# Moving a relay from SyncE to GpSimd and the loads and stores of GpSimd to SyncE, with longer DMA transposes and 4-byte taps, in a convolution + SwiGLU kernel

## The chip, the cores and the metric

One core of a Trainium2 chip. The metric is the device time of one execution in microseconds (us), lower is better.

## The reference, cut to what matters

```python
# x (8, 4096, 192), weight (8 heads, 7 taps); w_gate, w_val (192, 1536), w_out (1536, 192)
w = softmax(weight, axis=-1)
out = causal 7-tap convolution of x along the sequence, one filter per head of 24 channels
x = out.reshape(32768, 192)
g = x @ w_gate
return (g * sigmoid(g) * (x @ w_val)) @ w_out          # float32
```

## The kernel before

The 32768 rows are worked on in 64 blocks of 512 rows. Two blocks make a unit; 32 units. One unit has 24 steps (12 groups of 128 hidden columns, for each of two blocks). In each step PE does six matmuls (gate and val, 64 of its 128 rows each, in alternation), ACT does a Silu (g * sigmoid(g)), DVE multiplies. Between them stand bursts of matmuls that use the two halves ("row tiles") of the array for different banks of PSUM, the memory that takes PE's results: the out projection in two of three steps, and the convolution of the next unit in steps 0, 3, 6 and 9. After each burst the halves swap banks, and the first matmul of the next burst may only start when the last one is finished. This is what the relay is for: a no-op on another engine that waits for the last matmul and that the next burst waits for.

```python
    def after_relay(mm):
        last_mm[0] = mm
        if relay[0] is not None:
            tc.add_manual_dep(mm.ins, relay[0].ins.name, SYNC, reason="row tiles swap banks")
            relay[0] = None

    def emit_relay():
        relay[0] = nc.sync.nop(nofuse=True)
        tc.add_manual_dep(relay[0].ins, last_mm[0].ins.name, SYNC, reason="row tiles swap banks")
```

The convolved unit goes from SBUF (`stage`) to a DRAM scratch (`xc`) and comes back transposed (`xq`), 64 channels on each half of the partitions. Both are DMAs that SyncE issues, in program order with the relays. Loads of x (which cast to fp16 as they go) and stores of the output are issued by GpSimd. At the start, the filter taps are placed in `toep` ("toeplitz"), banded matrices with which PE does the convolution as matmuls.

```python
    def emit_to_dram(b):                       # the "scratch store"
        ...
        nc.sync.dma_start(out=dr.rearrange("(g r) d -> r g d", r=G), in_=conv[u][i * Q : i * Q + G])

    def emit_transpose(b, i):                  # six a block, RP = 256 rows each
        ...
        r, q = i // NQ * RP, i % NQ
        nc.sync.dma_start_transpose(
            out=xqs[b][:, q, r : r + RP], in_=drs[b][r : r + RP, q * Q : q * Q + P])
    ...
    # in the loop over steps s of a unit (cut):
        if burst and live:
            emit_relay()
        ...
            if s in (11, 12):
                emit_to_dram((u + 1) * UB + s - 11)
            if 17 <= s < 17 + 2 * NQ:
                emit_transpose((u + 1) * UB, s - 17)      # first block of the next unit
        if live and s < 2 * NQ:
            emit_transpose(u * UB + 1, s)                 # second block of this unit
```

Of the kernel before, what the change touches and what calls it, by code (L numbers as in the profile page):

```python
# [11 lines left out]
def kernel(  # L12
# [9 lines left out]
    nc = tc.nc  # L22
    fp32 = mybir.dt.float32
    fp16 = mybir.dt.float16
    i32 = mybir.dt.int32
    u16 = mybir.dt.uint16
    AF = mybir.ActivationFunctionType
    ALU = mybir.AluOpType
    AX = mybir.AxisListType
# [2 lines left out]
    B, S, D = x.shape  # L32
    H, K = weight.shape
    NT = B * S
    Dff = moe_w_gate.shape[1]
    P = 128
    grp = D // H
    SUBS = 4
    TB = P * SUBS
    NCH = Dff // P  # L40
    pad = K - 1

    Q = 64
    NQ = D // Q
    G = 57
    UG = 9
    UB = 2
# [1 line left out]
    XD = D + Q  # L49
    TR = 3  # L50
    F2_LAG = TR + 1
    RP = TB // 2
    SCALE = 1024.0

    assert D == NQ * Q and NQ == 3 and UB == 2 and UG * G >= TB
# [5 lines left out]
    n_units = NT // UT  # L61
    upb = S // UT

    x_flat = x.flatten_outer_dims()

    const_pool = ctx.enter_context(tc.tile_pool(name="const", bufs=1))
# [8 lines left out]


    last_rows = TB - ((UG - 1) * G - pad)
    x16s = []
    for i in range(2):
        x16 = const_pool.tile([P, UG, D], fp16, tag=f"x16_{i}", name=f"x16_{i}")  # L80
        nc.gpsimd.memset(x16[Q:P, UG - 1, :], 0.0)
        x16s.append(x16)

    def windows(t, rows, n):
        return bass.AP(
            tensor=x_flat.tensor, offset=t * D, ap=[[D, rows], [G * D, n], [1, D]]
        )

    def emit_fetch(u):
        x16 = x16s[u % 2]  # L90
        t0 = u * UT - pad
        if u % upb == 0:
            nc.gpsimd.memset(x16[0:pad, 0, :], 0.0)
            nc.gpsimd.dma_start(out=x16[pad:Q, 0, :], in_=x_flat[t0 + pad : t0 + Q, :])
            nc.gpsimd.dma_start(out=x16[0:Q, 1:UG, :], in_=windows(t0 + G, Q, UG - 1))
        else:
            nc.gpsimd.dma_start(out=x16[0:Q, :, :], in_=windows(t0, Q, UG))  # L97
        tb = t0 + TB
        nc.gpsimd.dma_start(  # L99
            out=x16[Q:P, 0 : UG - 1, :], in_=windows(tb, Q, UG - 1)  # L100
        )
        tl = tb + (UG - 1) * G
        nc.gpsimd.dma_start(  # L103
            out=x16[Q : Q + last_rows, UG - 1, :], in_=x_flat[tl : tl + last_rows, :]
        )

    man = tc.manual_schedule(engines={EN.PE, EN.SP, EN.Activation, EN.DVE, EN.Pool})
    ctx.enter_context(man)
# [4 lines left out]
        out=wraw, in_=bass.AP(tensor=weight.tensor, offset=0, ap=[[0, P], [K, H], [1, K]])  # L113
# [8 lines left out]
    FS = Dff // 4  # L122
    wg_v = moe_w_gate.rearrange("(q p) f -> p q f", p=Q)
    wv_v = moe_w_val.rearrange("(q p) f -> p q f", p=Q)
    wo_v = moe_w_out.rearrange("(c p) d -> p c d", p=P)
    for f in range(0, Dff, FS):
        fs = slice(f, f + FS)
        cs = slice(f // P, (f + FS) // P)
        nc.sync.dma_start(out=w_st[0:Q, :, fs], in_=wg_v[:, :, fs])
        nc.sync.dma_start(out=w_st[Q:P, 0 : NQ - 1, fs], in_=wv_v[:, 1:NQ, fs])  # L130
        nc.sync.dma_start(out=w_st[Q:P, NQ - 1, fs], in_=wv_v[:, 0, fs])
        nc.sync.dma_start(out=wo_st[:, cs, :], in_=wo_v[:, cs, :])


    diag = const_pool.tile([P, G], i32, tag="diag", name="diag")
    for lo in (0, Q):
        nc.gpsimd.iota(diag[lo : lo + Q], pattern=[[-1, G]], base=0, channel_multiplier=1)
    band = const_pool.tile([P, H, 2, G], fp16, tag="band", name="band")
    nc.gpsimd.memset(band, 0.0)
    toep = const_pool.tile([P, H, 2, P], fp16, tag="toep", name="toep")  # L140
    nc.gpsimd.memset(toep, 0.0)
    masks = []
    for k in range(K):
        mask = const_pool.tile([P, G], u16, tag=f"mask{k}", name=f"mask{k}")
        nc.vector.tensor_scalar(mask, diag, scalar1=k, scalar2=None, op0=ALU.is_equal)
        masks.append(mask)

# [17 lines left out]
    nc.vector.tensor_tensor(  # L165
        wn, wexp, wsum.unsqueeze(2).to_broadcast([P, H, K]), op=ALU.mult
    )
    whl = const_pool.tile([P, H, 2, K], fp16, tag="whl", name="whl")
    nc.vector.tensor_copy(whl[:, :, 0], wn)
    nc.vector.tensor_tensor(whl[:, :, 1], wn, whl[:, :, 0], op=ALU.subtract)  # L170
    for h in range(0, H, 4):
        hs = slice(h, h + 4)
        for k in range(K):
            nc.vector.copy_predicated(  # L174
                band[:, hs].rearrange("p h c m -> p (h c) m"),
                masks[k].unsqueeze(1).to_broadcast([P, 8, G]),
                whl[:, hs, :, k : k + 1]
                .rearrange("p h c k -> p (h c) k")
                .to_broadcast([P, 8, G]),
            )  # L180

        nc.vector.tensor_copy(toep[0:Q, hs, :, 0:G], band[0:Q, hs])  # L182
        nc.vector.tensor_copy(toep[Q:P, hs, :, Q : Q + G], band[Q:P, hs])

    def emit_weight_cast(i):
        fs = slice(i * FS, (i + 1) * FS)
        cs = slice(i * FS // P, (i + 1) * FS // P)
        nc.scalar.copy(w_r[:, :, fs], w_st[:, :, fs])
        nc.gpsimd.tensor_copy(wo_r[:, cs, :], wo_st[:, cs, :])

    emit_weight_cast(0)

    SYNC = mybir.DependencyInfo(mybir.DependencyClass.Sync, mybir.DependencyReason.DATA)
    relay = [None]
# [7 lines left out]

    def emit_relay():

        relay[0] = nc.sync.nop(nofuse=True)  # L205
        tc.add_manual_dep(
            relay[0].ins, last_mm[0].ins.name, SYNC, reason="row tiles swap banks"
        )
# [51 lines left out]

    xqs = {}

    def emit_transpose(b, i):

        if i == 0:
            xqs[b] = xpool.tile([P, NQ, TB], fp16, tag="xq", name="xq")
        r, q = i // NQ * RP, i % NQ
        nc.sync.dma_start_transpose(  # L268
            out=xqs[b][:, q, r : r + RP], in_=drs[b][r : r + RP, q * Q : q * Q + P]
        )  # L270

    def emit_gv(j, xq):
# [55 lines left out]
    def emit_store(b, acc):  # L328
        t0 = b * TB
        o_sb = opool.tile([P, SUBS, D], fp32, tag="o_sb", name="o_sb")  # L330
        nc.scalar.copy(o_sb[:, 0:2, :], acc[0])  # L331
        nc.vector.tensor_copy(o_sb[:, 2:4, :], acc[1])  # L332
        nc.gpsimd.dma_start(  # L333
            out=out[t0 : t0 + TB, :].rearrange("(s p) d -> p s d", p=P), in_=o_sb
        )

    for fill in range(2):
        for phase in range(2):
# [4 lines left out]
        if fill == 0:  # L343
            emit_dup(0)
    emit_to_dram(0)
    for i in range(2 * NQ):
        emit_transpose(0, i)
    emit_to_dram(1)
    for i in range(1, 4):
        emit_weight_cast(i)  # L350
    if n_units > 1:
        emit_fetch(1)

    hlists, accs = {}, {}
    ns = NCH * UB
    for g in range(n_blocks * NCH + F2_LAG):
        b, j = divmod(g, NCH)
# [28 lines left out]
        if burst and live:  # L386
            emit_relay()
        if g >= F2_LAG and fj == NCH - 2:
            emit_store(fb, accs.pop(fb))
        if live:  # L390
            emit_h(sj, ps, hlists[b])
        if g >= F2_LAG and fj == NCH - 1:
# [1 line left out]
        if more:  # L394
            if s in (3, 4, 9, 10):
                emit_conv_out(u + 1, s // 6, s % 3)
            if s == 5:
                emit_dup(u + 1)
                if u + 2 < n_units:
                    emit_fetch(u + 2)  # L400
            if s in (11, 12):
                emit_to_dram((u + 1) * UB + s - 11)
            if 17 <= s < 17 + 2 * NQ:
                emit_transpose((u + 1) * UB, s - 17)
        if live and s < 2 * NQ:
            emit_transpose(u * UB + 1, s)


# [28 lines left out]
```

## Time and profile before

| | before |
|---|---|
| time, median of 2 runs | 1077.84 us |
| first Silu | 41.2 us |
| one unit, mean (from first Silus of units 0 and 31, 41.19 and 1043.99 us) | 32.35 us |
| PE busy / mean granted clock | 84% / 0.987 |

The page's first part (busy us, share of the span, instructions):

```profile
PE 910.0 (84%) x11752; PEld 562.7 (52%) x11752; DVE 572.8 (53%) x865; ACT 550.1 (51%) x968; POOL 146.5 (14%) x222
```

No engine is full. The page's fourth part, the chain of waits, says who ended last, by engine and by line. SPq is SyncE's queue; L268 is the transpose, L255 the scratch store:

```profile
PE 43%; SPq 32%; DMA 8%; DVE 7%; issue 4%; ACT 4%; POOL 0%; POOLq 0%; ACTq 0%; DVEq 0%
SPq L268 24%; PE gate L278 17%; PE val L278 9%; SPq L255 8%; DVE h L294 4%; ACT sig L289 4%; DVE o_sb L332 2%; DVE band L174 1%; DMA xc_220<-stage 1%; DMA xc_229<-stage 1%; DMA xq<-xc_16634 0%; DMA xq<-xc_11455 0%; SPq L205 0%; DMA xq<-xc_6851 0%; DMA xq<-xc_6276 0%
```

The waits view (who waited for what: us in total, times, longest). L205 is the relay; PE's weight loads wait for it:

```profile
PEld L307 <- SPq L205: 145.4, 168, 3.1
...
PEld L227 <- SPq L205: 25.9, 56, 1.6
```

SyncE's queue in one unit, whose first Silu is at 431.59 and the next unit's at 463.19 (timeline: start, us, engine, line, what, count):

```profile
432.45 8.27 SPq L268 DMA_TRANSPOSE xq<-xc_6865  x6
446.16 0.25 SPq L255 DMA_DIRECT2D xc_7426<-stage  x1
446.46 2.60 SPq L255 DMA_DIRECT2D xc_7440<-stage  x1
453.69 7.89 SPq L268 DMA_TRANSPOSE xq<-xc_7426  x6
```

The transposes are read from the second block's store of the unit before (xc_6865) and from the first block's of the next (xc_7426). The last one of xc_7426 leaves SyncE at 461.58, 1.6 us before the unit begins that needs it. How long one holds SyncE (the view of a line: least, median, longest in ns):

```profile
L268 SPq DMA_TRANSPOSE xq<-xc_1095 x6: 1163/1204/1959, 98.4 to 105.8; - x6
```

The start, from the timeline: first convolution, its second half, scratch store, transposes, first gate matmul, first Silu:

```profile
15.35 0.36 PE L227 MATMUL cps_173<-x_0_82,toep 64*128 64x216 f16 x1 [15.35 <-DVE toep L182]
...
21.69 0.36 PE L227 MATMUL cps_196<-x_0_82,toep 64*128 64x216 f16 x1 [4.13 <-DVE toep L182]
...
25.01 0.34 SPq L255 DMA_DIRECT2D xc_220<-stage  x1
31.76 7.63 SPq L268 DMA_TRANSPOSE xq<-xc_220  x6
38.02 0.60 PE L278 MATMUL gate<-xq,w_sb 64*128 64x512 f16 x1 [14.12 <-DMA xq<-xc_220]
...
41.19 0.60 ACT L289 ACTIVATE sig<-gate 128x512 f16<-128x512 f32 x1 [13.13 <-PE val L278]
```

### The profile page before, as it was taken

The numbers are of one execution on the slowest core, as the hardware profiler recorded it, in microseconds if no ns is written. First come the engines' busy times: TensorE is split into PE (matmuls) and PEld (weight loads), VectorE is DVE, ScalarE is ACT, GpSimd is POOL, SyncE is SP. The second block draws the span as 40 slices with busy tenths as digits, with TensorE's granted clock in tenths as the row PEclk, the third lists the DMA queues.
The fourth block names the chain that finished last, engine by engine and source line by source line (L and its number), as shares of the span: only waits on it lengthen the run. The fifth ranks groups of instructions, "written<-read, shape, count | busy, mean of one in ns | idle before, by whom it ended". The sixth has DMA issues, their size and how long they took to land.

```text
span 1077.4 us, 28716 instructions
## 1 busy us (share of the span) xinstructions
PE 910.0 (84%) x11752; PEld 562.7 (52%) x11752; DVE 572.8 (53%) x865; ACT 550.1 (51%) x968; POOL 146.5 (14%) x222
## 2 busy tenths in 40 slices
PE   1488989888888888998888988888888888988887
PEld 0155655555555555655555555555555555655555
DVE  5155555555555555555555555455555555554555
ACT  2255555554555455555554555455555454554554
POOL 4001111110111101111100111101111101111000
PEclk9999999999999999999999999999999999999999
DMA  9424443423444335444423443333433423443321
GB/s 163 58 66 92 88 83 74 90 78 68 89 75 78 80 69 91 86 82 75 92 69 78 89 83 71 78 79 81 91 83 73 89 71 76 88 82 70 80 72 38
DMA packets 192916, 86.72 MB, mean 80 GB/s; under 512 B 150736, under 2 KB 187664, under 8 KB 192784
## 3 DMA queue, kind: packets, MB, share of 16 engines
q0 software_dynamic: 45696, 39.29, 20.5%
q1 hardware_dynamic: 147088, 45.59, 18.5%
q8 instruction: 92, 1.51, 0.6%
q14 instruction: 40, 0.33, 0.1%
HBM read 31.79 MB, written 41.98 MB: 68 GB/s over the span
## 4 chain that ended last, share of the span: by engine, by line
PE 43%; SPq 32%; DMA 8%; DVE 7%; issue 4%; ACT 4%; POOL 0%; POOLq 0%; ACTq 0%; DVEq 0%
SPq L268 24%; PE gate L278 17%; PE val L278 9%; SPq L255 8%; DVE h L294 4%; ACT sig L289 4%; DVE o_sb L332 2%; DVE band L174 1%; DMA xc_220<-stage 1%; DMA xc_229<-stage 1%; DMA xq<-xc_16634 0%; DMA xq<-xc_11455 0%; SPq L205 0%; DMA xq<-xc_6851 0%; DMA xq<-xc_6276 0%
## 5 line engine op out<-in xcount | busy, mean ns | idle before, releaser
L294 DVE TENSOR_TENSOR h<-sig,val 128x512 f16<-128x512 f16 x768 | 526.2, 687 | 443.5 <-ACT sig L289 386.2
L289 ACT ACTIVATE sig<-gate 128x512 f16<-128x512 f32 x768 | 458.5, 597 | 476.0 <-PE val L278 289.6
L278 PE MATMUL gate<-xq,w_sb 64*128 64x512 f16 x2304 | 645.6, 382 | 53.1 <-DMA xq<-xc_220 15.4
L278 PE MATMUL val<-xq,w_sb 64*128 64x512 f16 x2304 | 634.7, 380 | 18.1 <-DVE h L294 13.1
L307 PEld LDWEIGHTS <-h 64*128 64x128 f16 x6096 | 297.2, 95 | 198.7 <-SPq L205 145.4
L278 PEld LDWEIGHTS <-w_sb 64*128 64x128 f16 x4608 | 263.2, 95 | 250.7 <-issue 107.7
L333 POOL DMA_DIRECT2D out_dram<-o_sb x64 | 49.7, 777 | 855.9 <-ACT o_sb L331 462.0
L227 PEld LDWEIGHTS <-toep 64*128 64x128 f16 x1024 | 49.1, 97 | 59.1 <-SPq L205 25.9
L247 POOL COPY stage<-stage 128x576 f16<-128x576 f16 x32 | 21.5, 673 | 64.4 <-ACT stage L239 64.4
L227 PE MATMUL cps_173<-x_0_82,toep 64*128 64x216 f16 x8 | 1.9, 372 | 15.4 <-DVE toep L182 15.4
L97 POOL DMA_DIRECT2D x_1_84<-in_x_dram x16 | 12.2, 764 | 0.2 <-issue 0.2
L99 POOL DMA_DIRECT2D x_1_84<-in_x_dram x16 | 11.5, 718 | 0.0
L99 POOL DMA_DIRECT2D x_0_82<-in_x_dram x16 | 11.4, 711 | 0.0
L103 POOL DMA_DIRECT2D x_0_82<-in_x_dram x16 | 9.1, 566 | 0.0
L103 POOL DMA_DIRECT2D x_1_84<-in_x_dram x16 | 9.0, 562 | 0.2 <-issue 0.2
L307 PE MATMUL acc_325<-wo_sb,h 64*128 64x192 f16 x48 | 5.3, 243 | 3.2 <-SPq L205 3.2
L307 PE MATMUL acc_4067<-wo_sb,h 64*128 64x192 f16 x48 | 5.3, 243 | 2.9 <-SPq L205 2.9
L307 PE MATMUL acc_9246<-wo_sb,h 64*128 64x192 f16 x48 | 5.8, 258 | 2.1 <-SPq L205 2.1
L307 PE MATMUL acc_14425<-wo_sb,h 64*128 64x192 f16 x48 | 5.7, 256 | 2.1 <-SPq L205 2.1
L307 PE MATMUL acc_15577<-wo_sb,h 64*128 64x192 f16 x48 | 5.8, 258 | 1.8 <-SPq L205 1.8
L307 PE MATMUL acc_4642<-wo_sb,h 64*128 64x192 f16 x48 | 5.3, 243 | 2.4 <-SPq L205 2.4
L307 PE MATMUL acc_9821<-wo_sb,h 64*128 64x192 f16 x48 | 5.8, 258 | 1.4 <-SPq L205 1.4
(550 smaller groups left out, 975.5 us busy)
## 6 DMA issues: line engine op xcount, KB each, us to landing
out_dram<-o_sb POOLq DMA_DIRECT2D x64, 384.0 KB, 5.2
x_0_82<-in_x_dram POOLq DMA_DIRECT2D x24, 192.0 KB, 4.8
x_1_84<-in_x_dram POOLq DMA_DIRECT2D x16, 216.0 KB, 4.1
x_1_84<-in_x_dram POOLq DMA_DIRECT2D x16, 192.0 KB, 4.8
x_0_82<-in_x_dram POOLq DMA_DIRECT2D x8, 216.0 KB, 4.4
w_st<-in_moe_w_gate_dram SPq DMA_DIRECT2D x4, 288.0 KB
wo_st<-in_moe_w_out_dram SPq DMA_DIRECT2D x4, 288.0 KB
w_st<-in_moe_w_val_dram SPq DMA_DIRECT2D x4, 192.0 KB
```

Source lines behind the costliest of these rows:

```text
L99: nc.gpsimd.dma_start(out=x16[Q:P, 0 : UG - 1, :], in_=windows(tb, Q, UG - 1))
L103: nc.gpsimd.dma_start(out=x16[Q : Q + last_rows, UG - 1, :], in_=x_flat[tl : tl + last_rows, :])
L227: mm = nc.tensor.matmul(conv["ps"][a][:, :, e, :], toep[lo : lo + Q, h, c, :], x16[lo : lo + Q, :, h * grp : (h + 1) * grp], start=(phase ...
L247: nc.gpsimd.tensor_copy(conv[u][:, :, D:XD], conv[u][:, :, 0:Q])
L255: nc.sync.dma_start(out=dr.rearrange("(g r) d -> r g d", r=G), in_=conv[u][i * Q : i * Q + G],)
L268: nc.sync.dma_start_transpose(out=xqs[b][:, q, r : r + RP], in_=drs[b][r : r + RP, q * Q : q * Q + P])
L278: last_mm[0] = nc.tensor.matmul(ps[i], w_r[lo : lo + Q, q, ts(j, P)], xq[lo : lo + Q, q, :], start=(q == 0), stop=(q == NQ - 1),)
L289: nc.scalar.activation(sj, ps[0], AF.Silu)
L294: nc.vector.tensor_tensor(hj, sj, ps[1], op=ALU.mult)
L307: mm = nc.tensor.matmul(acc[a][:, i, :], hlist[j][lo : lo + Q, ts(2 * a + i, P)], wo_r[lo : lo + Q, j, :], start=(j == 0 and half == 0 and ...
L332: nc.vector.tensor_copy(o_sb[:, 2:4, :], acc[1])
L333: nc.gpsimd.dma_start(out=out[t0 : t0 + TB, :].rearrange("(s p) d -> p s d", p=P), in_=o_sb)
```

## The change

The intent is to take the relay out of the queue that issues DMAs. It goes to GpSimd, which then should not be busy with DMA issues; so loads and stores go to SyncE, and as a load from there does not cast (the prediction names the page for that), x lands as fp32 and GpSimd casts it in three pieces per unit. Each block has three transposes of 512 rows in place of six of 256. At the start, the high and low fp16 halves of each filter tap are placed as one 4-byte word (7 predicated copies in place of 14), half of the toeplitz copies go to ACT, weight loads come in two pieces in place of four, and the out weights are loaded from ACT's queue. Three further edits, of which the cut below shows the first: both blocks' transposes now go out in the unit before (steps 16 to 21); the second unit's x stands ahead of the first scratch store in SyncE's queue; and DVE in place of GpSimd clears the toeplitz tiles. The core of the diff:

```diff
 def emit_relay():
-        relay[0] = nc.sync.nop(nofuse=True)
+        relay[0] = nc.gpsimd.nop(nofuse=True)

 def emit_fetch(u):                                  # cut: four loads, all alike
-            nc.gpsimd.dma_start(out=x16[0:Q, :, :], in_=windows(t0, Q, UG))
+            nc.sync.dma_start(out=x32[0:Q, :, :], in_=windows(t0, Q, UG))
+def emit_x_cast(u, i):
+        gs = slice(i * UG // 3, (i + 1) * UG // 3)
+        nc.gpsimd.tensor_copy(x16s[u % 2][:, gs, :], x32s[u % 2][:, gs, :])

-    def emit_transpose(b, i):
-        r, q = i // NQ * RP, i % NQ
+    def emit_transpose(b, q):
         nc.sync.dma_start_transpose(
-            out=xqs[b][:, q, r : r + RP], in_=drs[b][r : r + RP, q * Q : q * Q + P]
+            out=xqs[b][:, q, :], in_=drs[b][0:TB, q * Q : q * Q + P]

-        nc.gpsimd.dma_start(out=out[...], in_=o_sb)
+        return lambda: nc.sync.dma_start(out=o_v, in_=o_sb)     # issued in steps 4 and 16

 # in the loop
-                    emit_fetch(u + 2)                # after the copy of step 5
+                if s == 6:
+                    emit_fetch(u + 2)
+                if 14 <= s < 17:
+                    emit_x_cast(u + 2, s - 14)
-            if 17 <= s < 17 + 2 * NQ: ...            # first block of the next unit
-        if live and s < 2 * NQ: ...                  # second block of this unit
+            if 16 <= s < 16 + UB * NQ:
+                emit_transpose((u + 1) * UB + (s - 16) // NQ, (s - 16) % NQ)

 # at the start
-    for h in range(0, H, 4): for k in range(K): nc.vector.copy_predicated(...)   # 14 of 456 fp16
-        nc.vector.tensor_copy(toep[Q:P, ...], ...)
+    for k in range(K): nc.vector.copy_predicated(band_w, ..., whl_w[...])        # 7 of 456 int32
+    for i in range(3): emit_x_cast(0, i)
+    emit_weight_cast(0); emit_weight_cast(1)         # ACT and GpSimd, wait for the weights
+        nc.scalar.copy(toep[Q:P, ...], ...)          # ACT, behind them
-        nc.sync.dma_start(out=wo_st[:, cs, :], in_=wo_v[:, cs, :])
+        nc.scalar.dma_start(out=wo_st[:, cs, :], in_=wo_v[:, cs, :])
```

More of the change, by code (lines that the diff above doesn't have):

```diff
@@ L25 @@
     i32 = mybir.dt.int32
-    u16 = mybir.dt.uint16
     AF = mybir.ActivationFunctionType
@@ L51 @@
     F2_LAG = TR + 1
-    RP = TB // 2
     SCALE = 1024.0
@@ L77 @@
     last_rows = TB - ((UG - 1) * G - pad)
-    x16s = []
+    x32s, x16s = [], []
     for i in range(2):
-        x16 = const_pool.tile([P, UG, D], fp16, tag=f"x16_{i}", name=f"x16_{i}")
-        nc.gpsimd.memset(x16[Q:P, UG - 1, :], 0.0)
-        x16s.append(x16)
+        x32 = const_pool.tile([P, UG, D], fp32, tag=f"x32_{i}", name=f"x32_{i}")
+        nc.gpsimd.memset(x32[Q:P, UG - 1, :], 0.0)
+        x32s.append(x32)
+        x16s.append(const_pool.tile([P, UG, D], fp16, tag=f"x16_{i}", name=f"x16_{i}"))
     def windows(t, rows, n):
@@ L89, in emit_fetch @@
     def emit_fetch(u):
-        x16 = x16s[u % 2]
+        x32 = x32s[u % 2]
         t0 = u * UT - pad
         if u % upb == 0:
-            nc.gpsimd.memset(x16[0:pad, 0, :], 0.0)
-            nc.gpsimd.dma_start(out=x16[pad:Q, 0, :], in_=x_flat[t0 + pad : t0 + Q, :])
-            nc.gpsimd.dma_start(out=x16[0:Q, 1:UG, :], in_=windows(t0 + G, Q, UG - 1))
+            nc.gpsimd.memset(x32[0:pad, 0, :], 0.0)
+            nc.sync.dma_start(out=x32[pad:Q, 0, :], in_=x_flat[t0 + pad : t0 + Q, :])
+            nc.sync.dma_start(out=x32[0:Q, 1:UG, :], in_=windows(t0 + G, Q, UG - 1))
         else:
-            nc.gpsimd.dma_start(out=x16[0:Q, :, :], in_=windows(t0, Q, UG))
+            nc.sync.dma_start(out=x32[0:Q, :, :], in_=windows(t0, Q, UG))
         tb = t0 + TB
-        nc.gpsimd.dma_start(
-            out=x16[Q:P, 0 : UG - 1, :], in_=windows(tb, Q, UG - 1)
-        )
-        tl = tb + (UG - 1) * G
-        nc.gpsimd.dma_start(
-            out=x16[Q : Q + last_rows, UG - 1, :], in_=x_flat[tl : tl + last_rows, :]
-        )
+        nc.sync.dma_start(out=x32[Q:P, 0 : UG - 1, :], in_=windows(tb, Q, UG - 1))
+        tl = tb + (UG - 1) * G
+        nc.sync.dma_start(
+            out=x32[Q : Q + last_rows, UG - 1, :], in_=x_flat[tl : tl + last_rows, :]
+        )
+    def emit_x_cast(u, i):
+        gs = slice(i * UG // 3, (i + 1) * UG // 3)
+        nc.gpsimd.tensor_copy(x16s[u % 2][:, gs, :], x32s[u % 2][:, gs, :])
     man = tc.manual_schedule(engines={EN.PE, EN.SP, EN.Activation, EN.DVE, EN.Pool})
@@ L125 @@
     wo_v = moe_w_out.rearrange("(c p) d -> p c d", p=P)
-    for f in range(0, Dff, FS):
-        fs = slice(f, f + FS)
-        cs = slice(f // P, (f + FS) // P)
+    for f in range(0, Dff, 2 * FS):
+        fs = slice(f, f + 2 * FS)
+        cs = slice(f // P, (f + 2 * FS) // P)
         nc.sync.dma_start(out=w_st[0:Q, :, fs], in_=wg_v[:, :, fs])
@@ L131 @@
         nc.sync.dma_start(out=w_st[Q:P, NQ - 1, fs], in_=wv_v[:, 0, fs])
-        nc.sync.dma_start(out=wo_st[:, cs, :], in_=wo_v[:, cs, :])
+        nc.scalar.dma_start(out=wo_st[:, cs, :], in_=wo_v[:, cs, :])
+    if n_units > 1:
+        emit_fetch(1)
     diag = const_pool.tile([P, G], i32, tag="diag", name="diag")
@@ L137 @@
         nc.gpsimd.iota(diag[lo : lo + Q], pattern=[[-1, G]], base=0, channel_multiplier=1)
-    band = const_pool.tile([P, H, 2, G], fp16, tag="band", name="band")
-    nc.gpsimd.memset(band, 0.0)
+    band = const_pool.tile([P, H, G, 2], fp16, tag="band", name="band")
+    nc.vector.memset(band, 0.0)
     toep = const_pool.tile([P, H, 2, P], fp16, tag="toep", name="toep")
-    nc.gpsimd.memset(toep, 0.0)
+    nc.vector.memset(toep, 0.0)
     masks = []
     for k in range(K):
-        mask = const_pool.tile([P, G], u16, tag=f"mask{k}", name=f"mask{k}")
+        mask = const_pool.tile([P, G], i32, tag=f"mask{k}", name=f"mask{k}")
         nc.vector.tensor_scalar(mask, diag, scalar1=k, scalar2=None, op0=ALU.is_equal)
@@ L167 @@
     )
-    whl = const_pool.tile([P, H, 2, K], fp16, tag="whl", name="whl")
-    nc.vector.tensor_copy(whl[:, :, 0], wn)
-    nc.vector.tensor_tensor(whl[:, :, 1], wn, whl[:, :, 0], op=ALU.subtract)
-    for h in range(0, H, 4):
-        hs = slice(h, h + 4)
-        for k in range(K):
-            nc.vector.copy_predicated(
-                band[:, hs].rearrange("p h c m -> p (h c) m"),
-                masks[k].unsqueeze(1).to_broadcast([P, 8, G]),
-                whl[:, hs, :, k : k + 1]
-                .rearrange("p h c k -> p (h c) k")
-                .to_broadcast([P, 8, G]),
-            )
-        nc.vector.tensor_copy(toep[0:Q, hs, :, 0:G], band[0:Q, hs])
-        nc.vector.tensor_copy(toep[Q:P, hs, :, Q : Q + G], band[Q:P, hs])
+    whl = const_pool.tile([P, H, K, 2], fp16, tag="whl", name="whl")
+    nc.vector.tensor_copy(whl[:, :, :, 0], wn)
+    nc.vector.tensor_tensor(whl[:, :, :, 1], wn, whl[:, :, :, 0], op=ALU.subtract)
+    band_w = band.rearrange("p h m c -> p h (m c)").bitcast(i32)
+    whl_w = whl.rearrange("p h k c -> p h (k c)").bitcast(i32)
+    for k in range(K):
+        nc.vector.copy_predicated(
+            band_w,
+            masks[k].unsqueeze(1).to_broadcast([P, H, G]),
+            whl_w[:, :, k : k + 1].to_broadcast([P, H, G]),
+        )
     def emit_weight_cast(i):
@@ L189, in emit_weight_cast @@
         nc.gpsimd.tensor_copy(wo_r[:, cs, :], wo_st[:, cs, :])
+    for i in range(3):
+        emit_x_cast(0, i)
     emit_weight_cast(0)
+    emit_weight_cast(1)
+    for h in range(0, H, 4):
+        hs = slice(h, h + 4)
+        bv = band[:, hs].rearrange("p h m c -> p h c m")
+        nc.vector.tensor_copy(toep[0:Q, hs, :, 0:G], bv[0:Q])
+        nc.scalar.copy(toep[Q:P, hs, :, Q : Q + G], bv[Q:P])
     SYNC = mybir.DependencyInfo(mybir.DependencyClass.Sync, mybir.DependencyReason.DATA)
@@ L261 @@
     xqs = {}
-    def emit_transpose(b, i):
-        if i == 0:
+    def emit_transpose(b, q):
+        if q == 0:
             xqs[b] = xpool.tile([P, NQ, TB], fp16, tag="xq", name="xq")
-        r, q = i // NQ * RP, i % NQ
         nc.sync.dma_start_transpose(
-            out=xqs[b][:, q, r : r + RP], in_=drs[b][r : r + RP, q * Q : q * Q + P]
+            out=xqs[b][:, q, :], in_=drs[b][0:TB, q * Q : q * Q + P]
         )
@@ L332, in emit_store @@
         nc.vector.tensor_copy(o_sb[:, 2:4, :], acc[1])
-        nc.gpsimd.dma_start(
-            out=out[t0 : t0 + TB, :].rearrange("(s p) d -> p s d", p=P), in_=o_sb
-        )
+        o_v = out[t0 : t0 + TB, :].rearrange("(s p) d -> p s d", p=P)
+        return lambda: nc.sync.dma_start(out=o_v, in_=o_sb)
     for fill in range(2):
@@ L345 @@
     emit_to_dram(0)
-    for i in range(2 * NQ):
-        emit_transpose(0, i)
+    for q in range(NQ):
+        emit_transpose(0, q)
     emit_to_dram(1)
-    for i in range(1, 4):
+    for i in range(2, 4):
         emit_weight_cast(i)
+    for q in range(NQ):
+        emit_transpose(1, q)
     if n_units > 1:
-        emit_fetch(1)
-    hlists, accs = {}, {}
+        for i in range(3):
+            emit_x_cast(1, i)
+    hlists, accs, stores = {}, {}, []
     ns = NCH * UB
@@ L388 @@
         if g >= F2_LAG and fj == NCH - 2:
-            emit_store(fb, accs.pop(fb))
+            stores.append(emit_store(fb, accs.pop(fb)))
         if live:
@@ L398 @@
                 emit_dup(u + 1)
-                if u + 2 < n_units:
+            if u + 2 < n_units:
+                if s == 6:
                     emit_fetch(u + 2)
+                if 14 <= s < 17:
+                    emit_x_cast(u + 2, s - 14)
             if s in (11, 12):
                 emit_to_dram((u + 1) * UB + s - 11)
-            if 17 <= s < 17 + 2 * NQ:
-                emit_transpose((u + 1) * UB, s - 17)
-        if live and s < 2 * NQ:
-            emit_transpose(u * UB + 1, s)
+            if 16 <= s < 16 + UB * NQ:
+                emit_transpose((u + 1) * UB + (s - 16) // NQ, (s - 16) % NQ)
+        if s % NCH == 4 and stores or not live:
+            for st in stores:
+                st()
+            stores.clear()
 _INS = ['x', 'weight', 'moe_w_gate', 'moe_w_val', 'moe_w_out']
```

## The prediction

> **What bounds the kernel now.** A unit (two 512-token blocks, 24 steps) takes about 32 us: starts of the Silu at the unit boundaries stand at 76.7, 108.7, 139.2 us (timeline). Neither PE nor another engine is full: PE 84%, DVE 53%, ACT 51% (page). From the timeline, one step of gate/val matmuls is 0.65 us and one burst of half-array matmuls 0.49 us (1.14 us where both stand); the ring PE, Silu 0.60, product 0.69, PE holds a burst-free step to about 0.87. Undisturbed that adds up to some 26.5 us a unit. The missing 5.5 us are SyncE's queue: the chain of waits gives 24% of the span to the transposes' line and 8% to the store to the DRAM scratch. SyncE runs the relay (burst, no-op, next burst) in order with its DMA issues. Each 256x128 transpose holds it 1.18 to 1.24 us, six per block, and the second scratch store 2.6 us; relays behind them come late (PE weight loads wait 145 + 26 us for the relay, in the waits view). And the first block's transposes begin only at step 17, since relays stand before them in the queue (98.4 to 107 us in the second unit), so the next block waits for the landing (2.4 us after the last issue).
>
> **What the change does.**
> - Relay on GpSimd. The Trainium skill, page "DMA: Bandwidth & Descriptors", section "Constraints" under "DMA Transpose (X-bar)", says that a plain DMA transpose comes only from the SP/ACT queues; so the relay has to move, not the transposes. GpSimd then carries one copy (0.67 us), three casts (estimate 0.7 to 0.9 us each, from the 128x576 weight casts) and the relays, placed so that a cast falls after its step's relay. I expect almost no relay wait.
> - SyncE is free to run ahead: the transposes start when the scratch store has landed (about step 15) and not at step 17. It gains three x loads and two output stores per unit (about 0.6 to 0.75 us each) and issues 3 instead of 6 transposes per block. If issue time goes with rows, a 512-row one costs 2.0 to 2.4 us, so nothing is saved there. Sum about 20 us of 27 per unit: fits, but the first block's last transpose lands close to its need; I allow 0.5 to 1 us of wait a unit.
> - GpSimd's DMA issues vanish (about 100 us of its 146 busy); they were off the critical path. "SWDGE vs HWDGE vs iDMA" on the same page: a cast within a DMA is only GpSimd's, hence the separate casts. Fetched bytes double in SBUF; DMA is 39% busy, no limit.
> - Start: 7 predicated copies of 456 four-byte elements in place of 14 (0.64 us each) save about 4.5 us, but the toeplitz copies on ACT now stand behind two weight casts that wait for larger weight loads. First gate matmul from 38.0 to about 33 to 35 us; first Silu 41.2 to about 37.5.
>
> **Sum.** 37.5 + 31 x 27.3 + 25 for the last unit (no convolution) + 8 of tail + rounding: about 920 us, ratio 0.85. Range 890 to 965. Faster 0.96, same 0.03, slower 0.01.
>
> **What would show it.** Unit period 26.5 to 28 us; waits for the relay under 40 us in all; transposes and scratch stores nearly gone from the chain of waits, with PE, ACT and DVE in their place; transpose issue 2.0 to 2.4 us; PE share over 90%; DVE 60%.
>
> **What would make it wrong.** GpSimd's semaphore path slower than SyncE's by more than the 0.65 us that hide it: 500 relays would each add to the time. A cast waiting for its load, with relays behind it, since loads queue behind six transposes. 512-row transposes costing over 2.6 us, so that every block's start waits. GpSimd casts slowing the product on DVE.

## The result, and the profile after

| | before | after |
|---|---|---|
| time, median | 1077.84 us (2 runs) | 904.19 us (2 runs) |
| ratio | | 0.839 (95% interval 0.828 to 0.850) |
| first Silu | 41.2 us | 42.2 us |
| one unit, mean | 32.35 us | 26.73 us |
| PE busy / granted clock | 84% / 0.987 | 93% / 1.000 |

Ratios here and below are the mean time of one kernel's fast runs over that of the other's of the same rounds, so not quite the ratio of the medians that are quoted.

The time falls by 173.65 us; 31 units at 32.35 - 26.73 = 5.62 us are 174 us. So the whole gain lies in the repeated part, and the start gave nothing. Page part one and the chain of waits (L275 is the transpose now, L285 gate and val):

```profile
PE 835.8 (93%) x11752; PEld 635.0 (70%) x11752; DVE 566.6 (63%) x858; ACT 552.6 (61%) x970; POOL 88.9 (10%) x148
```

```profile
PE 70%; DVE 14%; ACT 7%; DMA 5%; issue 2%; SPq 1%; POOLq 0%; ACTq 0%
```

SyncE's queue went from 32% of the chain to 1%. The relay (L213 now) has nearly vanished from the waits; the view of its line, where it lists who waited for it (us, times):

```profile
who waited for it (us, times):
  PEld L235: 1.0, 2
```

SyncE in one unit (first Silus of this unit and the next: 364.4 and 391.0):

```profile
376.67 0.28 SPq L263 DMA_DIRECT2D xc_7377<-stage  x1
377.00 2.65 SPq L263 DMA_DIRECT2D xc_7391<-stage  x1
382.55 2.37 SPq L275 DMA_TRANSPOSE xq<-xc_7377  x1
385.03 0.53 SPq L341 DMA_DIRECT2D out_dram<-o_sb  x1
385.61 2.57 SPq L275 DMA_TRANSPOSE xq<-xc_7377  x2
388.29 3.81 SPq L275 DMA_TRANSPOSE xq<-xc_7391  x3
```

The first transpose starts 5.9 us after the scratch store is issued, when it has landed (18.2 us after the unit's first Silu, in step 16). The three transposes of the next block are out at 388.2, 5.6 us after the first began; before, six took 7.9. Why is plain from the line's view (a median of 1.27 us here, 1.20 in the unit shown before): a transpose of twice the rows holds SyncE hardly longer.

```profile
L275 SPq DMA_TRANSPOSE xq<-xc_507 x3: 1257/1271/1651, 61.8 to 65.5; - x3
```

GpSimd's three casts stand in steps 14 to 16 and are short:

```profile
380.89 1.28 POOL L106 CAST x_0_84<-x_0_82 128x576 f16<-128x576 f32 x2 [9.18 <-PE acc_7183 L314]
383.26 0.67 POOL L106 CAST x_0_84<-x_0_82 128x576 f16<-128x576 f32 x1 [1.09 <-PE acc_7471 L314]
```

The start after (x cast, weight cast, ACT's toeplitz copies, second row half of the first convolution, scratch store, transposes, first gate matmul, first Silu):

```profile
16.57 1.88 POOL L106 CAST x_0_84<-x_0_82 128x576 f16<-128x576 f32 x3 [14.65 <-DMA x_0_82<-in_x_dram]
...
22.15 2.20 ACT L186 CAST w_sb<-w_st 128x1152 f16<-128x1152 f32 x2 [14.22 <-DMA w_st<-in_moe_w_val_dram]
24.38 1.05 ACT L199 COPY toep<-band 64x456 f16<-64x456 f16 x2
...
25.01 0.36 PE L235 MATMUL cps_169<-x_0_84,toep 64*128 64x216 f16 x1 [6.18 <-ACT toep L199]
...
30.90 0.28 SPq L263 DMA_DIRECT2D xc_215<-stage  x1
...
36.44 3.83 SPq L275 DMA_TRANSPOSE xq<-xc_215  x3
39.09 0.58 PE L285 MATMUL gate<-xq,w_sb 64*128 64x512 f16 x1 [9.25 <-DMA xq<-xc_215]
...
42.20 0.60 ACT L296 ACTIVATE sig<-gate 128x512 f16<-128x512 f32 x1 [9.13 <-PE val L285]
```

### The profile page after: what moved, and what is told of

It is laid out like the page before. It is cut to its first block, busy times and chain, and to the rows that moved or that the text cites. A ratio compares the mean times of both kernels' runs of the same rounds, so it can differ in the third digit from the quotient of the medians.

```text
span 902.4 us, 28501 instructions
## 1 busy us (share of the span) xinstructions
PE 835.8 (93%) x11752; PEld 635.0 (70%) x11752; DVE 566.6 (63%) x858; ACT 552.6 (61%) x970; POOL 88.9 (10%) x148
## 3 DMA queue, kind: packets, MB, share of 16 engines
q8 instruction: 92, 1.51, 0.7%
q10 hardware_dynamic: 1568, 1.18, 0.5%
## 4 chain that ended last, share of the span: by engine, by line
PE 70%; DVE 14%; ACT 7%; DMA 5%; issue 2%; SPq 1%; POOLq 0%; ACTq 0%
PE val L285 34%; DVE h L301 11%; PE gate L285 8%; ACT sig L296 6%; DVE o_sb L339 4%; DMA w_st<-in_moe_w_val_dram 1%; DMA wo_st<-in_moe_w_out_dram 1%; SPq L275 1%; DMA xc_215<-stage 1%; DMA xq<-xc_13675 1%; DMA xq<-xc_507 1%; DMA xq<-xc_3369 1%; DMA xq<-xc_4515 0%; DMA xq<-xc_215 0%; ACT w_sb L186 0%
## 5 line engine op out<-in xcount | busy, mean ns | idle before, releaser
L285 PE MATMUL val<-xq,w_sb 64*128 64x512 f16 x2304 | 622.7, 376 | 24.8 <-DVE h L301 16.8
L285 PE MATMUL gate<-xq,w_sb 64*128 64x512 f16 x2304 | 631.1, 378 | 11.9 <-DMA xq<-xc_215 10.5
L285 PEld LDWEIGHTS <-w_sb 64*128 64x128 f16 x4608 | 322.0, 94 | 180.8 <-issue 89.5
L314 PEld LDWEIGHTS <-h 64*128 64x128 f16 x6096 | 370.3, 94 | 44.4
L235 PEld LDWEIGHTS <-toep 64*128 64x128 f16 x1024 | 73.2, 95 | 37.3 <-DVE toep L198 13.2
L255 POOL COPY stage<-stage 128x576 f16<-128x576 f16 x32 | 21.3, 667 | 441.7 <-PE acc_314 L314 16.2
L106 POOL CAST x_0_84<-x_0_82 128x576 f16<-128x576 f32 x48 | 31.1, 668 | 164.6 <-DMA x_0_82<-in_x_dram 14.7
L106 POOL CAST x_1_87<-x_1_85 128x576 f16<-128x576 f32 x48 | 31.1, 667 | 153.1 <-PE gate L285 9.4
L235 PE MATMUL cps_168<-x_0_84,toep 64*128 64x216 f16 x8 | 2.0, 372 | 18.5 <-POOL x_0_84 L106 18.5
L186 ACT CAST w_sb<-w_st 128x1152 f16<-128x1152 f32 x4 | 4.4, 1148 | 14.2 <-DMA w_st<-in_moe_w_val_dram 14.2
L235 PE MATMUL cps_169<-x_0_84,toep 64*128 64x216 f16 x8 | 1.8, 377 | 6.3 <-ACT toep L199 6.2
L314 PE MATMUL acc_4036<-wo_sb,h 64*128 64x192 f16 x48 | 5.2, 243 | 0.0
L314 PE MATMUL acc_8042<-wo_sb,h 64*128 64x192 f16 x48 | 5.2, 243 | 0.0
L314 PE MATMUL acc_10045<-wo_sb,h 64*128 64x192 f16 x48 | 5.2, 243 | 0.0
L314 PE MATMUL acc_16630<-wo_sb,h 64*128 64x192 f16 x48 | 5.2, 243 | 0.0
L314 PE MATMUL acc_600<-wo_sb,h 64*128 64x192 f16 x48 | 5.2, 243 | 0.0
L314 PE MATMUL acc_2890<-wo_sb,h 64*128 64x192 f16 x48 | 5.2, 243 | 0.0
L314 PE MATMUL acc_2891<-wo_sb,h 64*128 64x192 f16 x48 | 5.2, 243 | 0.0
L314 PE MATMUL acc_6326<-wo_sb,h 64*128 64x192 f16 x48 | 5.2, 243 | 0.0
L314 PE MATMUL acc_6898<-wo_sb,h 64*128 64x192 f16 x48 | 5.2, 243 | 0.0
```

What stands on the lines that cost most here:

```text
L106: nc.gpsimd.tensor_copy(x16s[u % 2][:, gs, :], x32s[u % 2][:, gs, :])
L186: nc.scalar.copy(w_r[:, :, fs], w_st[:, :, fs])
L235: mm = nc.tensor.matmul(conv["ps"][a][:, :, e, :], toep[lo : lo + Q, h, c, :], x16[lo : lo + Q, :, h * grp : (h + 1) * grp], start=(phase ...
L255: nc.gpsimd.tensor_copy(conv[u][:, :, D:XD], conv[u][:, :, 0:Q])
L285: last_mm[0] = nc.tensor.matmul(ps[i], w_r[lo : lo + Q, q, ts(j, P)], xq[lo : lo + Q, q, :], start=(q == 0), stop=(q == NQ - 1),)
L314: mm = nc.tensor.matmul(acc[a][:, i, :], hlist[j][lo : lo + Q, ts(2 * a + i, P)], wo_r[lo : lo + Q, j, :], start=(j == 0 and half == 0 and ...
```

## The experiments

Twelve kernels ran, all correct. One table serves for most of them. It gives the mean time from the Silu of one step to the next, over units 1 to 30, worked out from the Silus' starts in the timeline; only steps that differ by much are shown. Step 23 is the one that ends with the first Silu of the next unit.

| step | before | relay alone (e1) | 512 rows alone (e2) | after, relay back (e3) | after, 256 rows (e4) | both in before (e5) | after |
|---|---|---|---|---|---|---|---|
| 0 | 1.18 | 1.55 | 1.01 | 1.02 | 1.69 | 1.01 | 1.01 |
| 1 | 1.27 | 1.59 | 1.14 | 1.14 | 1.75 | 1.14 | 1.14 |
| 7 | 1.56 | 1.94 | 1.14 | 1.14 | 1.14 | 1.94 | 1.14 |
| 8 | 1.14 | 1.14 | 1.14 | 1.84 | 1.14 | 1.14 | 1.14 |
| 14 | 1.88 | 1.14 | 1.96 | 1.93 | 1.14 | 1.14 | 1.14 |
| 20 | 2.24 | 1.14 | 1.95 | 2.66 | 1.14 | 1.14 | 1.14 |
| 23 | 3.59 | 4.26 | 1.16 | 2.16 | 4.26 | 1.22 | 1.23 |
| whole unit | 32.24 | 31.47 | 28.48 | 30.52 | 31.03 | 27.45 | 26.67 |
| time | 1078 | 1048 | 957 | 1032 | 1046 | 922 | 904 |

### e1: the relay alone

```diff
 # kernel before
-        relay[0] = nc.sync.nop(nofuse=True)
+        relay[0] = nc.gpsimd.nop(nofuse=True)
```

> The kernel before with one line changed: the relay is a no-op on GpSimd; transposes stay 256 rows, loads and stores stay on GpSimd. Theory A (the relay's place in SyncE's queue costs most of it): unit 28 to 29.5 us, 935 to 980 us, since the transposes may start early but are still 12 a unit, and GpSimd's own DMA issues (0.6 to 0.8 us each, the store waiting for its copies) stand before a few relays. Rival B (the number of transposes costs it): little gain, 1030 us or more. Rival C (GpSimd cannot carry the relay while it issues DMAs): no gain or slower, 1060 us or more, with the relay waits now on GpSimd's queue.

Measured: 1048.13 us, ratio 0.971 (0.968 to 0.975). A miss for theory A: 30 us of the 174; rival B's forecast (1030 us or more) came in. Steps 14 and 20, where relays stood behind SyncE's stores and transposes, fall to their bare 1.14 us. But step 23 grows to 4.26: PE waits for the landing of the transposes (86.7 us by gate matmuls in all, in the waits view), because twelve a unit are still issued one after the other behind the scratch store. With the relay out of the way the first of them starts 20.0 us into the unit in place of 22.0, but the six then take 9.8 in place of 8.5 us (means over units 2 to 30). A part of the loss is the PE clock: its mean over e1's runs is 0.962 (before, 0.982), and steps 0 and 1 together take 0.7 us more than before. Rival C is refuted in its strong form: GpSimd carries the relay. It does pay in step 7, where three of its own load issues stand before a relay.

### e2: 512-row transposes alone

```diff
 # kernel before, six emissions a block -> three, in the first three of the six places
-        out=xqs[b][:, q, r : r + RP], in_=drs[b][r : r + RP, q * Q : q * Q + P]
+        out=xqs[b][:, i, :], in_=drs[b][0:TB, i * Q : i * Q + P]     # if i < NQ
```

> The kernel before with three 512-row transposes a block in place of six of 256 rows; relay still on SyncE. Each should cost SyncE about 1.26 us as after. Theory A: SyncE still delays relays, but less; 960 to 1010 us. Rival B: nearly all of the gain, 900 to 930 us.

Measured: 957.35 us, ratio 0.888 (0.885 to 0.891). It is the larger part by far: 121 us with the relay where it was. Step 23 is down to 1.16. What is left are relays behind the scratch store (step 14) and behind transposes (step 20); weight loads still wait for the relay 77.3 + 12.4 us. Theory A's range (960 to 1010) was missed at its lower end and rival B's (900 to 930) too: both costs are real, and the count of transposes is the bigger.

### e3: the changed kernel with the relay back on SyncE

```diff
 # changed kernel
-        relay[0] = nc.gpsimd.nop(nofuse=True)
+        relay[0] = nc.sync.nop(nofuse=True)
```

> The changed kernel with one line undone: the relay back on SyncE, where loads, stores and 512-row transposes now all stand. Theory A: 970 to 1030 us, relay waits of 100 us or more by SyncE. Rival B: 900 to 930 us.

Measured: 1032.00 us, 128 us more than the change. It differs from e2 in that SyncE also issues loads (step 8) and stores and all six transposes of a unit in a row (steps 20 and 23), and that costs 75 us over e2. Some 5 of the 75 are a later start (first Silu at 42.5, in e2 at 37.8). The time is 2 us above theory A's range; the weight loads wait for the relay as it expected:

```profile
PEld L314 <- SPq L213: 146.6, 134, 2.5
```

The Trainium skill, page "DMA: Bandwidth & Descriptors", section "Issuing engines are not separate DMA queues", says that issuing DMAs from several engines saves only the sequencer's time to start them, "which is usually small relative to the DMA itself". In this kernel that time is what counts, since the same sequencer passes PE's relay: the DMAs are the same in number and size in the change and in e3, and 128 us lie between them.

### e4: the changed kernel with 256-row transposes

```diff
 # changed kernel, each transpose in two
+        for r in (0, TB // 2):
             nc.sync.dma_start_transpose(
-            out=xqs[b][:, q, :], in_=drs[b][0:TB, q * Q : q * Q + P])
+            out=xqs[b][:, q, r : r + TB // 2], in_=drs[b][r : r + TB // 2, q * Q : q * Q + P])
```

> The changed kernel with each transpose split in two of 256 rows (12 a unit on SyncE, about 1.2 us each), relay on GpSimd. Theory A with a tight chain (scratch store, transposes, landing): the first block's transposes end about 3.5 us later than the 26.6 us unit allows less a slack of about 1 us, so the unit is 27.5 to 29 us and the time 930 to 975 us, with waits for the transposes' landing at the start of each unit's first block. Rival (SyncE has slack enough): 904 us within 1%.

Measured: 1045.83 us, 142 us more than the change and more than expected. The theory's direction holds, its slack was mis-sized: step 23 takes 3.0 us more than in the change. The timelines of SyncE and of PE at the end of one unit show the chain, store issued at 437.92, landed by 443.81, where the first transpose starts, then six transposes (the sixth ends at 452.92; the view merges it with later ones), landing, PE:

```profile
437.92 2.90 SPq L263 DMA_DIRECT2D xc<-stage  x2
443.81 3.11 SPq L276 DMA_TRANSPOSE xq<-xc  x2
447.03 0.52 SPq L343 DMA_DIRECT2D out_dram<-o_sb  x1
447.93 9.38 SPq L276 DMA_TRANSPOSE xq<-xc  x7
```

```profile
454.07 0.37 PE L287 MATMUL gate<-xq,w_sb 64*128 64x512 f16 x1 [1.90 <-DMA xq<-xc]
...
456.36 0.63 PE L287 MATMUL gate<-xq,w_sb 64*128 64x512 f16 x1
```

The second PE line shows the rest of the loss: 2.3 us after the wait the same matmul takes 0.63 in place of 0.37 us. The windows view has the granted clock in its column after the engines (start and end, busy of each engine, clock, DMA share, GB/s), and it falls after the wait:

```profile
448.00:451.00 3.00, 2.95 (x44) 2.05 (x41) 1.90 (x4) 1.71 (x3) 0.00 (x0) 1.00 0.65 178
...
454.00:457.00 3.00, 2.93 (x32) 2.15 (x33) 1.38 (x2) 1.19 (x2) 0.00 (x0) 0.70 0.22 49
```

This fits steps 0 and 1, which are 1.3 us longer together. The Trainium skill, page "TensorE: Matmul & The Clock Gate", section "What's actually happening", says that too little activity throttles the PE clock and that activity releases it; the trace agrees, with 0.70 after this wait and 0.948 over the whole run, against 1.000 in the change.

The trace's clock records and PE's busy time say more. Every stretch at the lower clock in e4 has a clock of 0.50, and all 27 begin on one grid of 3.41 us. Here PE was busy for 1.51 of the 3.41 us from 451.77 to 455.18, and from 455.18 to 458.60 the clock was 0.50. In this run, from 51 us on, such a stretch followed only slots of the grid in which PE was busy 11 to 49%; the slots after which the clock stayed at 1.00 were busy 46% at the least. In the kernel before the two groups are 20 to 46% and 51% or more; in e1 they overlap a little (22 to 54%, 51% or more). So in these runs what counted was whether PE was busy about half of a slot; this is inferred from busy times, which the profile in part models.

The chain can also be followed through all runs. Means over units 2 to 30, us from a unit's first Silu:

| | before | e1 | e4 | e5 | after |
|---|---|---|---|---|---|
| scratch store of the next unit's first block issued | 14.5 | 14.1 | 13.6 | 13.1 | 12.3 |
| its first transpose starts | 22.0 | 20.0 | 19.8 | 19.0 | 18.2 |
| its last transpose has left SyncE | 30.5 | 29.8 | 29.3 | 24.6 | 23.5 |
| next unit's first Silu | 32.3 | 31.6 | 31.1 | 27.5 | 26.7 |

Between the last two rows lie 1.8 us in each of the three kernels with 256 rows, but 2.9 and 3.1 us in e5 and the change: the chain sets the unit in the three and has room (an estimate: 1.1 to 1.3 us) in the other two.

### e5: relay and 512 rows, nothing else

The edits of e1 and e2 in the kernel before; loads, casts in the DMA, stores and start as before.

> The kernel before with both edits of the first two runs: relay on GpSimd and 512-row transposes; loads and stores still DMA issues of GpSimd. Alone they gave -30 and -121 us. Theory A2 (two bounds in series: relays behind SyncE's issues, and the chain scratch store, transposes, landing; the step that is left bounds alone): more than their sum of 151 us is not expected, the unit falls to the bare 26.6 us plus the steps where GpSimd's own issues stand before a relay (step 7 took 1.97 in place of 1.14 us in the first run), so about 27.5 to 28 us, 915 to 945 us. Rival C (moving the DMAs off GpSimd is needed for the gain): 960 us or more. If 904 within 1%: the moved DMAs and casts are worth nothing.

Measured: 922.27 us, ratio 0.855 (0.852 to 0.858), as theory A2 expected. The two edits give 156 us together, 30 and 121 alone (5 us more than the sum, which A2 did not expect; the runs of the kernel before lie 13 us apart in these rounds). The unit differs from the change only in step 7, 1.94 against 1.14 us, where GpSimd's three load issues stand before a relay:

```profile
346.40 0.77 POOL L97 DMA_DIRECT2D x<-in_x_dram  x1
347.16 0.72 POOL L99 DMA_DIRECT2D x<-in_x_dram  x1
347.85 0.56 POOL L103 DMA_DIRECT2D x<-in_x_dram  x1
```

So moving the DMAs off GpSimd is worth 0.78 us a unit, some 24 us in 31 units. The first Silu of e5 comes at 35.8 us and that of the change at 42.2, so the changed start gives 6.4 us back. The two make 18 us, which is what lies between 922.27 and 904.19.

### e6: the 4-byte taps alone

```diff
 # kernel before; all toeplitz copies stay on DVE
-    14 copy_predicated of 456 fp16 with uint16 masks, band [P, H, 2, G]
+    7 copy_predicated of 456 int32 words, band [P, H, G, 2] and its taps read as int32
```

> The kernel before with only the taps placed as one 4-byte word: 7 predicated copies in place of 14, all toeplitz copies on DVE. Theory S (before, the start was bound by these copies): the first convolution still near 15 us, the second half at about 16 in place of 21.7, first gate matmul at 32 to 34 in place of 38.0 us; time 3 to 6 us less, 1072 us. Rival (bound by the loads): first gate matmul at 37 to 38.5 us, no change.

Measured: 1078.48 us, ratio 1.000 (0.996 to 1.003). A miss: the copies were on the way, but not what ended last. The scratch store is issued 2.9 us sooner than before (25.01) and lands no sooner (before, the transposes began at 31.76):

```profile
22.09 0.34 SPq L255 DMA_DIRECT2D xc<-stage  x1
31.89 6.34 SPq L268 DMA_TRANSPOSE xq<-xc  x5
```

### e7 and e8: ACT's order at the start, and the out weights later

```diff
 # e7: changed kernel
-    three x casts; emit_weight_cast(0); emit_weight_cast(1); toeplitz copies (half on ACT)
+    toeplitz copies (half on ACT); three x casts; all weight casts after the first convolution
 # e8: e7, and
-        nc.scalar.dma_start(out=wo_st[:, cs, :], ...)       # first thing, ACT's queue
+        nc.sync.dma_start(out=wo_st[:, cs, :], ...)         # after gate and val, before the second x
```

> The changed kernel with ACT's queue reordered at the start: toeplitz copies first, all four weight casts after the convolution of the first unit. Theory S2 (the start gained nothing because ACT's toeplitz copies stood behind two weight casts that waited for the weights until 22.15 us): convolution begins at about 18.5 (x casts) in place of 25.0, first gate matmul at 31 to 33 in place of 39.1, time 6 to 8 us less: 896 to 898 us. Rival (landing of the scratch store behind the weight loads bounds): first gate matmul at 37 us or later, under 2 us gained.

> As the run before, and the loads of the out weights no longer issued first thing from ACT's queue but from SyncE's after the other weights. If they delayed the first x loads (x casts began at 16.57 us): x casts at 9 to 12 us, convolution at about 14, first gate matmul at 28 to 31 us, a further 2 to 4 us less, 892 to 895 us. Rival: no difference to the run before.

Measured: e7 902.54 us, e8 905.67 us (the change 904.19). Both theories miss; the rival of e7, landing behind the loads, is nearly right. ACT was what held up the second row half of the first convolution (25.01 in the change; in e7 the first 16 convolution matmuls run from 17.80 to 19.71), but the first gate matmul comes only at 36.9 and the first Silu at 40.2. In e7 the store is issued at 23.70, 7.2 us sooner than in the change, and its transposes start at 34.25, only 2.2 us sooner. Ahead of it in SyncE's queue stands the load of the second unit's x, which lands at 29.53 (GpSimd's cast waits for it):

```profile
29.53 1.90 POOL L106 CAST x<-x 128x576 f16<-128x576 f32 x3 [4.20 <-DMA x<-in_x_dram]
```

```profile
23.70 0.28 SPq L260 DMA_DIRECT2D xc<-stage  x1
34.25 3.83 SPq L272 DMA_TRANSPOSE xq<-xc  x3
```

In e8 the first step of the theory does hold: the first x is cast from 9.11 us on (15.87 in e7). But SyncE is held by the issue of the second x until 24.78, so that the store is issued at 24.89 only, these loads land later still (the same cast starts at 32.00), and the transposes start at 36.67. In both the store lands 4.7 us after the load that stands last before it.

### e9 and e10: a relay that takes longer

```diff
 # changed kernel; 576 columns (e9) or 128 columns (e10) of fp16
-        relay[0] = nc.gpsimd.nop(nofuse=True)
+        relay[0] = nc.gpsimd.tensor_copy(junk[:, 0, 0:n], junk[:, 1, 0:n])
```

> The changed kernel with the relay's no-op replaced by a copy on GpSimd of 128x576 fp16 elements (0.67 us, as the copy inside the unit took), so that each of some 20 relays a unit is late by about 0.6 us. Theory (relay hidden behind one step's gate and val matmuls, 0.65 us): exposed where bursts follow in the very next step, some 16 gaps a unit by 0.1 to 0.4 us each, so 28 to 33 us a unit, 950 to 1080 us. Rival (the gap is not what hides it, other waits end later): within 2% of 904 us.

> The same with a copy of 128x128 elements, an estimate of 0.15 to 0.25 us by scaling. Theory: still hidden, 904 us within 1%. Rival (each relay already sits at the edge): 16 gaps by 0.15 us and more, 970 us or more.

Measured: e9 1078.41 us, with 0.667 us a copy; e10 926.04 us, with 0.293 us a copy. The unit is 32.21 and 27.39 us. e9 confirms that the relay is hidden only by the gate and val matmuls of one step: made late by 0.67 us some 20 times a unit, it takes the whole gain of the change back, at one end of the range expected. e10 misses "hidden, within 1%": it costs 22 us. The copy was longer than estimated, and the relay has less slack than the 0.29 us it added in some of the steps (5, 14, 17 and 19 were 0.2 us longer each, and 18 was 0.2 shorter), in most it has that much. That a copy on GpSimd slows DVE instead is excluded: the product takes 686 ns on the mean in e9, e10 and the change.

### e11: a start that keeps late loads behind the scratch store

```diff
 # changed kernel; ACT order as e7, and on SyncE's queue
-    all weights; second x; [scratch store 0; 3 transposes; scratch store 1; 3 transposes]
+    first half of gate, val; second x; first half of out weights;
+    [scratch stores 0, 1; 3 transposes]; the other halves; [3 transposes]
+    # casts of the other halves at steps 4, 6 (ACT) and 7, 8 (GpSimd) of the first block
```

> The changed kernel with its start reordered: ACT's queue as in the earlier run, and on SyncE only what the first steps need stands before the first scratch stores (first x, first half of gate and val weights, second x, first half of out weights); the rest is loaded after the first block's transposes and cast inside the loop. Theory S3 (the scratch store lands when the loads issued before it have drained, 31.8 us before, whatever the time of its issue): the store is issued at 18 to 20 and lands within 6 us, first gate matmul at 26 to 29 us in place of 39.1, first Silu at about 30, time 890 to 896 us. Rival (landing not set by the loads ahead): first gate matmul at 35 us or later.

Measured: 896.70 us, ratio to before 0.830 (0.829 to 0.831): it beats both kernels, with the same unit (26.79). The first gate matmul is at 31.9 and the first Silu at 33.7 us, later than expected (26 to 29) and sooner than the rival says. The store's issue, with its neighbour's, now takes 5.9 us, and the transposes start 3.8 us after the last load ahead (the out weights) had landed at 23.34:

```profile
23.34 1.28 POOL L193 CAST wo_sb<-wo_st 128x576 f16<-128x576 f32 x2 [7.43 <-DMA wo_st<-in_moe_w_out_dram]
```

```profile
18.17 5.92 SPq L266 DMA_DIRECT2D xc<-stage  x2
27.16 4.35 SPq L278 DMA_TRANSPOSE xq<-xc  x3
```

So theory S3 holds in kind: e7, e8 and e11 land 4.7, 4.7 and 3.8 us after the last load ahead of them. A part of the 8.5 us gained at the first Silu is given back within the first unit, which takes 30.1 us here and 28.6 in the change.

### e12: 128-row transposes, one look

```diff
 # changed kernel, each transpose in four of 128 rows
+        for r in range(0, TB, TB // 4): ...
```

> The changed kernel with each transpose split in four of 128 rows, one look. If a transpose's issue costs the same whatever its rows (1.26 us for 512, 1.24 for 256): 24 a unit, 1.2 us each, 36 us or more a unit, 1170 us or more. If issue goes with rows below 256: 0.6 to 0.7 us each, about as the split in two, 1046 us.

Measured: 1506.87 us (one run, state unknown; the mean granted clock is 0.829). The first forecast, 1170 us or more, holds, but the unit of 45.5 us is far above its 36: 16.2 us stand in step 23, and no run was made to split that. The line's view of this kernel, and that of e4:

```profile
L276 SPq DMA_TRANSPOSE xq<-xc x768: 1096/1230/3843, 36.7 to 1483.6; - x192
```

```profile
L276 SPq DMA_TRANSPOSE xq<-xc x384: 1103/1240/2602, 37.4 to 1019.6; - x192
```

At 128, 256 and 512 rows the median issue is 1.23, 1.24 and 1.26 us: in this range it goes by the instruction and not by the rows. The means are a little higher, 1.31, 1.35 and 1.44 us, since some take longer, above all the first of a unit (1.87 us on the mean in the change).

## Why the prediction was right or wrong

The time was right: 920 us said, 904.19 measured, inside 890 to 965. The sum was made of a start, 31 units, a last unit and a tail: 37.5 + 31 x 27.3 + 25 + 8. Measured: 42.2 + 31 x 26.73 + 25.0 (870.8 to 895.9 us) + 6.5 = 902.4, the profiled span. But the reason given for the unit was in good part wrong, so the number is partly luck.

- **Right: the bare unit of 26.5 us.** The ring of PE, Silu and product with bursts, read from undisturbed stretches of the trace before, is what remained: 26.73 us. Steps with an out-projection burst take 1.14 us nearly everywhere, as read.
- **Right: a relay behind SyncE's DMA issues is late, and GpSimd removes that.** The weight loads' waits for the relay fell from 171 us (145.4 + 25.9) to 1.0, steps 14 and 20 to 1.14 us. The casts after their step's relay delayed nothing (steps 14 and 16 are at 1.14 us, and the product on DVE, which it feared they might slow, takes 686 ns on the mean, 687 before). (That transposes come only from the SP and ACT queues, and casting DMAs only from GpSimd, is the Trainium skill's word, cited in the prediction; no run here tried otherwise.) The rider, that the 0.65 us of a step hide the relay, was too generous: e10 shows that 0.29 us more already shows.
- **Wrong: "If issue time goes with rows, a 512-row one costs 2.0 to 2.4 us, so nothing is saved there."** It does not go with rows: a median of 1.26 us against 1.18 before. This term was mis-sized by a factor of 1.6 to 1.9, and it is the largest saving of the change: 121 of 174 us when it is made alone (e2), 142 us when it alone is undone (e4). e4, where 512 rows cost 2 x 1.24 = 2.48 us of issue, is close to the kernel that the prediction described, and it took 1045.83 us, far outside the range. The prediction held because a second error went the other way.
- **Wrong: "the first block's last transpose lands close to its need; I allow 0.5 to 1 us of wait a unit", and the transposes start "about step 15".** They start in step 16, 18.2 us into the unit, since the scratch store takes 5.9 us to land. And in e4 the six, with an output store and gaps between them, take from 443.81 to 452.92 us, 9.1 us (9.5 on the mean of units 2 to 30), where three at 2.0 to 2.4 us would be 6 to 7.2. That leaves 3.0 us more in step 23 and a lower PE clock after it, 4.4 us a unit, not 0.5 to 1.
- **Wrong in weight: the relay as the main cause.** Alone it gives 30 us (e1), because the chain scratch store, transposes, landing bounded the unit at 31.5 us right behind it, and the clock fell. On top of the longer transposes it gives 35 us (e2 to e5). In the changed kernel it cannot be left out (e3: +128 us), for there SyncE carries all DMA issues.
- **Right in kind, with no size given: GpSimd's DMA issues were "off the critical path".** True of before (POOLq has 0% of the chain); but once the relay stands in their queue they cost 0.8 us a unit (e5, step 7), so their move was needed for 24 us of the gain.
- **Wrong: the start, "first gate matmul from 38.0 to about 33 to 35 us; first Silu 41.2 to about 37.5".** Measured 39.1 and 42.2. Two causes: the toeplitz copies on ACT waited behind the weight casts until 24.38 us, which the prediction named and sized too low, and the scratch store lands only some 4 to 5 us after the loads ahead of it, which it did not see. In the change itself the first binds (the transposes start 5.5 us after the store's issue, about the steady 5.9). With the first mended alone the second binds (e7: 40.2), and the saved predicated copies are worth nothing in the kernel before (e6).

What stays open: why the six transposes of e1 and e4 take 9.5 to 9.8 us where those of the kernel before take 8.5 (in e1 the first alone takes 2.8 in place of 1.5); and whether the 3.8 to 4.7 us between the last load's landing and the store's are the store's own latency or the draining of the queue, since no run issued the first store with nothing ahead of it.

## What to carry to other kernels

Count the instructions in a queue that also passes a signal of the critical path, and give each its issue time: making six DMA transposes into three longer ones was worth more than moving the signal, since each held the queue 1.2 to 1.3 us (median) at 128, 256 and 512 rows. When two waits lie close behind each other, undo each part in the changed kernel and also make each alone; the sums differ (30 and 121 us alone, 128 and 142 us when undone), and only both show the order of the bounds. A relay hidden behind other work has only that work's time as slack: 0.29 us more on each cost 22 us here, 0.67 us the whole gain.

## What the Trainium skill lacked or had wrong

- "DMA: Bandwidth & Descriptors" has a figure per transpose instruction for small tiles on generations before trn3, and no issue time by rows. These runs: 1.23 us at 128 rows, 1.24 at 256, 1.26 at 512, each with 128 columns of fp16 (medians on SyncE's queue).
- The same page, "Issuing engines are not separate DMA queues", calls the sequencer's time to start a DMA usually small. Here it was 12 x 1.2 us of a 32 us unit, and taking the relay out of that queue was worth 128 us (e3 against the change).
- "TensorE: Matmul & The Clock Gate" ("What's actually happening") puts throttling after an idle window of about 3.4 us. In e4 no such idle window was needed: the granted clock fell to 0.50 after slots of 3.41 us in which PE was busy up to 49%, as after the wait of 1.90 us that is shown.
- No page that was looked up gives the time from issue to landing of a 256 KB store to DRAM that SyncE issues (it belongs to "DMA: Bandwidth & Descriptors"): 5.9 us in the steady state here, read from the start of the transposes that wait for it, and behind loads 3.8 to 4.7 us after the last of them has landed.
